# Relative attention with a max-of-three layer on one core: the first tiles between the bias groups, a new place for the weight conversion, another count of products with v

## The chip, the cores and the metric

The kernel runs on one core of one Trainium2 chip. The metric is the device time of one execution in microseconds, as the median of several runs; the profile is one such execution.

## The reference

Four batches, eight heads, 576 positions, head dimension 64. A small network of 32 hidden units makes a bias for each pair of positions and each head; attention with that bias is followed by a layer that takes the largest of three products.

```python
scores = scale * np.matmul(q, k.transpose(0, 1, 3, 2))
x = (np.log1p(np.abs(rel)) / psi_i)[..., None]
bias = np.maximum(x @ w1 + b1, 0.0) @ w2                 # 576 x 576 x 8
attn = softmax(scores + bias)                            # over the last axis
out = np.matmul(attn, v)                                 # 4 x 8 x 576 x 64
...
h = np.maximum(np.maximum(x @ w1, x @ w2), x @ w3)       # 2304 x 768, x = out as 2304 x 512
return h @ w_out                                         # 2304 x 512
```

## The kernel before

The program is written out in one order by hand; each engine runs its own instructions in that order, and waits where an operand or a buffer is not ready. It has three stages.

**Bias.** 36 groups `g` of 16 rows. `hidden(g)` writes four tiles `hid` (three or four on VectorE, at most one on ScalarE, chosen by a running estimate `load`), `product(g - 1)` multiplies them on TensorE into a PSUM tile `bp`, and `finish` scales that into `bs` on ScalarE or VectorE and writes it to DRAM (`bias_d`). `bp` shares the PSUM tag `s` (two buffers) with the score tiles; `bs` has eight buffers. All DMAs go through SyncE's queue, in order: the write of each group, the reads `load_bias` of five bias tiles (`bias0` to `bias3` with 128 rows, and `biasm` with the last 64) when their groups are written, and the loads of q, k and v. The reads are issued at g = 10, 18, 26 and 34 and after the last group.

**Attention.** A unit is a pair of heads of one batch (16 units); a unit has five tiles t = 0 to 4, the last with one head's width. `step(n)` issues, in this order: `front(n)` (scores of tile n of `sched`, 12 matmuls, 6 for t = 4, into two `s` tiles), some queued products with v, `shift` (VectorE: scores plus bias, and their minimum) and `expo` (ScalarE: exponent and sum) for each head, `norm(n - 1)` (VectorE: a reciprocal; POOL: the scaling of e), for t = 0 and 1 a part of `prep` for the next unit (k, then q: a cast to the high part on ScalarE, `kh`/`qh`, and the rest on POOL, `kl`/`ql`), `split_x`, and `flip(n - 5)` (TensorE transposes of e, copied out by ScalarE and VectorE as `et`). Steps 0 to 4 thus have no flip. After tiles 1 and 4 of a unit five pairs of products with v are queued (group 0 over tiles 0 and 1, group 1 over tiles 2 to 4); steps with n mod 5 = 0, 1, 2, 3, 4 issue 3, 2, 2, 2, 1 of them. The accumulator `pv` has a single PSUM buffer. `split_x` copies a finished `pv` into `xhi` and `xlo` on VectorE, two instructions; the first pair of a new group calls it as well. Step 0 stands behind the last bias group, steps 1 to 84 after the bias stage.

**Max of three.** From 345 us on, matmuls with weights that `convert` has turned from double precision to two parts, with seven VectorE instructions per weight tile. The first three weight tiles (`load_w(..., 0)`) are converted during attention: from step 23 on, each third step advances the conversion by two pieces, behind the flip's copies.

Of the kernel before, what the change touches and what calls it, by code (L numbers as in the profile page):

```python
# [19 lines left out]
def kernel(  # L20
# [66 lines left out]
    def bias_stage(pool):  # L87
# [41 lines left out]
        for g in range(NG + 1):  # L129
            if g < NG:  # L130
                hidden(g)
            if g:
                product(g - 1)
            for x in range(max(g - 2, 0), g if g == NG else g - 1):
                finish(pool, k, load, x, late.pop(x))
            yield
# [33 lines left out]
    TS = 2  # L170
    sched = [(un, t) for un in range(len(units)) for t in range(NS)]
    NSTEP = len(sched)
    LAG = NS

    class Attention:
        def __init__(self, pool):
            self.pool = pool
            self.data = {}
            self.st = {}
            self.et = {}  # L180
            self.pvq = []
            self.done = []
            self.vl = [pool.tile([128, 2, D], F32, name=f"vl{x}", bufs=1) for x in range(2)]
# [14 lines left out]
        def prep(self, un):  # L198
            pool, u = self.pool, self.data[un]
            for w in "kq":  # L200
# [4 lines left out]
                nc.scalar.copy(hi, r)  # L205
                nc.gpsimd.tensor_tensor(out=lo, in0=r, in1=hi.bitcast(F32), op=ALU.subtract)
                yield
# [12 lines left out]
        def heads(self, n):  # L220
            return 2 if sched[n][1] < NTQ else 1

        def front(self, n):
            un, t = sched[n]
            pool, u = self.pool, self.data[un]
# [15 lines left out]
        def shift(self, n, h):  # L241
            un, t = sched[n]
            pool, st = self.pool, self.st[n]
# [9 lines left out]
        def expo(self, n, h):  # L253
            pool, st = self.pool, self.st[n]
            if h == 0:
                st["e"] = pool.tile([128, 2 * S], F32, tag="e", bufs=NS + 1, name=f"e{n}")
                st["sm"] = pool.tile([128, 2], F32, tag="sm", bufs=NS + 1, name=f"sm{n}")
            sn, nm = st.pop(h)
# [6 lines left out]
        def norm(self, n):  # L265
            st, nh = self.st[n], self.heads(n)
            sm = st["sm"][:, 0:nh]
            rc = self.pool.tile([128, 2], F32, tag="rc", bufs=NS + 1, name=f"rc{n}")
            nc.vector.reciprocal(rc[:, 0:nh], sm)  # L269
# [5 lines left out]
        def flip(self, n):  # L275
            un, t = sched[n]
            pool, e2 = self.pool, self.st[n]["e"]
            g = 0 if t < TS else 1
# [7 lines left out]
            tps = []  # L286
            for h in range(self.heads(n)):
                tp = ps_t(f"tp{un}_{t}_{h}")
# [47 lines left out]
        def step(self, n, more=None):  # L336
            m, f = n - 1, n - LAG
            nh = 0
            if n < NSTEP:
                un, t = sched[n]  # L340
                hp, b = units[un]
                if t == 0 and un + 2 < len(units):
                    self.load_qk(un + 2)
                if t == 2 and un:
                    self.load_v(un)
                nh = self.heads(n)
                self.front(n)
            for _ in range((3, 2, 2, 2, 1)[n % NS]):
                if self.pvq:
                    self.pvq.pop(0)()  # L350
            back = 0 <= f < NSTEP
            for h in range(nh):
# [12 lines left out]
            if back:  # L365
# [3 lines left out]
                if len(tps) > 1:  # L369
                    nc.vector.tensor_copy(*tps[1])  # L370
            if more is not None:
                for _ in range(2):
                    next(more, None)
            if back:
                un, t = sched[f]
                g = 0 if t < TS else 1
                w = 128 * TS if g == 0 else S - 128 * TS
                del self.st[f]
                if t in (TS - 1, NS - 1):
                    self.queue_pv(un, 128 * TS * g, w, *self.et)  # L380


    def convert(pool, src, hi, lo, name):
        n = src.shape[1] * src.shape[2] // 2
# [28 lines left out]
    def load_w(pool, wpool, f):  # L413
        for i, m in enumerate((mw1, mw2, mw3)):
# [3 lines left out]
            src = m[:, 256 * f:256 * f + 256].rearrange("(c p) f -> p c f", p=128)  # L418
            yield from convert(wpool, src, hi, lo, f"{i}_{f}")

# [71 lines left out]
    with tc.manual_schedule():  # L492
# [9 lines left out]
        with tc.tile_pool(name="bias_p", bufs=1) as bp:  # L502
            for g, _ in enumerate(bias_stage(bp)):
# [17 lines left out]
        xlo.extend(xpool.tile([128, NT], F32R, name=f"xlo{i}") for i in range(HP))  # L521
        w0 = load_w(wpool, wpool, 0)
# [66 lines left out]
```

## Time and profile before

| | |
|---|---|
| median of three runs | 643.92 us (643.84 to 645.93) |
| the profiled execution, own time | 646.02 us |
| its span, first to last instruction | 644.2 us |
| TensorE busy | 610.4 us |
| VectorE, ScalarE, POOL busy | 382.5, 297.3, 164.4 us |

The profiled execution took 2.1 us more than the median, and 1.8 us of its time lie outside the span. TensorE is busy in 95% of the span. From 345 us on it has no idle time to speak of; the idle time lies in the bias stage, in the first steps of attention and in the waits of its units.

### The profile page before, as it was taken

To read this page: it belongs to the slowest core of one execution; us is meant where nothing else is said; L and a number is where in the kernel's file an instruction comes from. 1 tells how busy PE (TensorE), PEld (TensorE's weight loads), DVE (VectorE), ACT (ScalarE), POOL (GpSimd) and SP (SyncE) were. 2 spreads that over 40 slices of the span, in tenths; PEclk is the share of its full clock that TensorE was granted. 3 is DMA by queue.
4 is the path that set the end of the run, shared out by engine and by line. 5 is a ranking of instruction groups with operands and counts; after the bars stand their busy time and mean duration, and the time that the engine had idled before them with its cause. 6 is when DMAs were issued, how large, how long until landed. Compare 5 with 4: busy or idle time off the path is not lost.

```text
span 644.2 us, 11473 instructions
## 1 busy us (share of the span) xinstructions
PE 610.4 (95%) x4248; PEld 464.2 (72%) x4248; DVE 382.5 (59%) x948; ACT 297.3 (46%) x788; POOL 164.4 (26%) x186
## 2 busy tenths in 40 slices
PE   8987799999899989999999999999999999999998
PEld 4324566666566666666666898989889898988886
DVE  7985466666686777678644474646646473233331
ACT  7977677776767667768651000000000001034443
POOL 2403555555556556656430000000000000000000
PEclk9989699999899999999999999999999999999999
DMA  5868323632264224510011111212212110001111
GB/s 166 274 234 291 108 60 102 180 88 59 52 180 138 61 62 132 173 33 19 20 33 34 34 65 44 75 46 67 65 34 83 48 66 0 1 34 66 66 65 67
DMA packets 47863, 55.16 MB, mean 86 GB/s; under 512 B 21952, under 2 KB 31424, under 8 KB 47808
## 3 DMA queue, kind: packets, MB, share of 16 engines
q1 hardware_dynamic: 47808, 54.43, 27.4%
q8 instruction: 34, 0.56, 0.4%
q14 instruction: 21, 0.17, 0.1%
HBM read 38.81 MB, written 15.61 MB: 84 GB/s over the span
## 4 chain that ended last, share of the span: by engine, by line
PE 72%; ACT 14%; DVE 6%; issue 4%; DMA 2%; POOL 1%; SPq 0%; DVEq 0%; ACTq 0%
PE pv L320 10%; PE h L461 8%; PE h L462 8%; PE h L463 8%; PE tp L291 7%; PE s L237 6%; ACT e L259 6%; PE g L462 4%; PE g L463 4%; PE g L461 4%; PE o L486 4%; PE o L485 4%; PE o L487 4%; ACT bs L144 2%; ACT et L367 2%
## 5 line engine op out<-in xcount | busy, mean ns | idle before, releaser
L259 ACT ACTIVATE e<-sn,nm 128x576 f32<-128x576 f32 x144 | 110.8, 770 | 70.5 <-DVE nm L247 54.3
L272 POOL TENSOR_SCALAR e<-e,rc 128x576 f32<-128x576 f32 x144 | 106.9, 755 | 99.4 <-DVE rc L269 66.6
L468 ACT COPY m<-h 128x512 f32<-128x512 f32 (+1 forms) x30 | 16.3, 544 | 206.1 <-PE h L463 187.2
L247 DVE CUSTOM_DVE_ANT_0 sn<-s,bias 128x576 f32<-128x576 f32 x128 | 91.8, 754 | 28.8 <-PE s L237 28.8
L320 PE MATMUL pv<-et,vt 128*64 128x320 f32 (+1 forms) x512 | 78.1, 420 | 15.8 <-ACT et L367 15.6
L463 PE MATMUL h<-xhi,wl 128*128 128x512 f32 (+1 forms) x240 | 88.3, 368 | 0.0
L461 PE MATMUL h<-xhi,wh 128*128 128x512 f32 (+1 forms) x240 | 88.2, 368 | 0.0
L462 PE MATMUL h<-xlo,wh 128*128 128x512 f32 (+1 forms) x240 | 88.2, 368 | 0.0
L291 PEld LDWEIGHTS tp<-ident,e 128*128 128x128 f32 x576 | 63.1, 143 | 34.1 <-issue 22.5
L291 PE MATMUL tp<-ident,e 128*128 128x128 f32 x576 | 82.3, 285 | 0.0
L370 DVE COPY et<-tp 128x512 f32<-128x512 f32 x64 | 44.0, 687 | 54.2 <-PE tp L291 52.0
L237 PE MATMUL s<-kh,qh 64*128 64x288 f32 (+1 forms) x288 | 64.1, 352 | 8.2 <-DVE nm L247 7.4
L320 PEld LDWEIGHTS pv<-et,vt 128*64 128x64 f32 x512 | 34.6, 136 | 39.5 <-ACT et L367 23.3
L237 PE MATMUL s<-kl,qh 64*128 64x288 f32 (+1 forms) x288 | 53.6, 305 | 0.0
L237 PEld LDWEIGHTS s<-kh,qh 64*128 64x128 f32 (+1 forms) x288 | 35.7, 190 | 23.4 <-DVE nm L247 12.3
L237 PE MATMUL s<-kh,ql 64*128 64x288 f32 (+1 forms) x288 | 51.7, 297 | 0.0
L367 ACT COPY et<-tp 128x512 f32<-128x512 f32 x80 | 45.8, 573 | 9.3 <-PE tp L291 9.3
L440 DVE TENSOR_TENSOR hl<-ht,hh 128x128 fp32r<-128x128 f32 x108 | 23.4, 285 | 44.9 <-ACT hh L439 44.9
L461 PEld LDWEIGHTS h<-xhi,wh 128*128 128x128 f32 x240 | 45.1, 188 | 6.2 <-issue 0.5
L469 DVE TENSOR_TENSOR m<-h,m 128x512 f32<-128x512 f32 (+1 forms) x30 | 19.1, 638 | 50.9 <-ACT m L468 50.8
L462 PEld LDWEIGHTS h<-xlo,wh 128*128 128x128 f32 x240 | 45.0, 188 | 5.7
L463 PEld LDWEIGHTS h<-xhi,wl 128*128 128x128 f32 x240 | 45.0, 188 | 5.6
(75 smaller groups left out, 1058.3 us busy)
## 6 DMA issues: line engine op xcount, KB each, us to landing
bias_d<-bs SPq DMA_DIRECT2D x36, 295.5 KB, 5.2
bias<-bias_d SPq DMA_DIRECT2D x16, 576.0 KB, 3.9
w<-in_moe_w_dram SPq DMA_DIRECT2D x18, 512.0 KB, 3.5
qr<-in_qd_dram SPq DMA_DIRECT2D x16, 320.0 KB, 3.1
kr<-in_kd_dram SPq DMA_DIRECT2D x16, 320.0 KB, 3.7
out_dram<-ot SPq DMA_DIRECT2D x17, 256.0 KB, 2.0
vt<-in_v_dram SPq DMA_DIRECT2D x32, 128.0 KB, 2.5
w64o<-in_moe_w_out_dram SPq DMA_DIRECT2D x6, 512.0 KB, 3.2
```

The source lines that it names most:

```text
L237: nc.tensor.matmul(ss[h][:, x, 0:HALF], lhsT=u[q][p, r], rhs=u[k][p, c:c + HALF], start=(j == 0), stop=(j == 2))
L247: nc.vector.tensor_tensor_reduce(out=sn.rearrange("p (a b) -> p a b", a=2), in0=st["s"][h][:, :, 0:HALF], in1=bt.rearrange("p (a b) -> p a ...
L259: nc.scalar.activation(st["e"][:, S * h:S * h + S], sn, ACTF.Exp, scale=-1.0, bias=nm, accum_out=st["sm"][:, h:h + 1])
L272: nc.gpsimd.tensor_scalar(out=e, in0=e, scalar1=rc[:, h:h + 1], scalar2=1.0, op0=ALU.mult, op1=ALU.mult)
L291: nc.tensor.transpose(tp[:, 128 * c:128 * c + 128], e2[:, k0:k0 + 128], ident)
L320: nc.tensor.matmul(pv[p], lhsT=w, rhs=x, start=(c == 0), stop=(c == NTQ))
L367: nc.scalar.copy(*tps[0])
L370: nc.vector.tensor_copy(*tps[1])
L461: nc.tensor.matmul(o, lhsT=hi[:, r], rhs=x, start=(c == 0), stop=False)
L462: nc.tensor.matmul(o, lhsT=hi[:, r], rhs=y, start=False, stop=False)
L463: nc.tensor.matmul(o, lhsT=lo[:, r], rhs=x, start=False, stop=(c == KDM - 1))
L485: nc.tensor.matmul(po, lhsT=hh[:, f], rhs=woh[:, f, r], start=(f == 0), stop=False)
```

## The change

Three tiles of unit 0 are issued between bias groups, behind g = 17, 25 and 33 (`AMID`); there `finish` also takes the group just multiplied. The steps follow a new list `fronts`: tiles 0, 1, 2 of unit 0, then tiles 0, 1, 2 of unit 1, then tiles 3 and 4 of unit 0, then 3 and 4 of unit 1, and so on in the old order. `flip` keeps the old order. So step 3 stands behind the last bias group, and steps 3 and 4 alone come after it without a flip. `norm` makes up for the first steps two at a time from step 3 on. `prep` computes the low parts of units 0 and 1 on VectorE; that of unit 1 stands in steps 1 and 2, that of unit 2 as a whole in step 8. Products with v are issued 1, 3, 2, 2, 2 per step. The conversion of the first weights advances by one piece in steps with n mod 5 of 2, 3 and 4 from step 20 on, right behind `expo`, and its last two pieces go to ScalarE and POOL. e has eight buffers instead of six, and v is loaded a tile later.

```diff
-            for x in range(max(g - 2, 0), g if g == NG else g - 1):
-                finish(pool, k, load, x, late.pop(x))
+            for x in sorted(late):
+                if x < g - 1 or g in AMID or g == NG:
+                    finish(pool, k, load, x, late.pop(x))
...
+    AMID = (17, 25, 33)
+    fronts = [sched[x] for x in (0, 1, 2, 5, 6, 7, 3, 4)] + sched[8:]
...
                 nc.scalar.copy(hi, r)
-                nc.gpsimd.tensor_tensor(out=lo, in0=r, in1=hi.bitcast(F32), op=ALU.subtract)
+                eng = nc.vector if un < 2 else nc.gpsimd
+                eng.tensor_tensor(out=lo, in0=r, in1=hi.bitcast(F32), op=ALU.subtract)
...
-                st["e"] = pool.tile([128, 2 * S], F32, tag="e", bufs=NS + 1, name=f"e{n}")
+                st["e"] = pool.tile([128, 2 * S], F32, tag="e", bufs=NS + 3, name=f"e{n}")
...
-            m, f = n - 1, n - LAG
+            f = n - LAG
             nh = 0
             if n < NSTEP:
-                un, t = sched[n]
+                un, t = fronts[n]
...
-                if t == 2 and un:
+                if t == 3 and un:
                     self.load_v(un)
...
-            for _ in range((3, 2, 2, 2, 1)[n % NS]):
+            for _ in range((1, 3, 2, 2, 2)[n % NS]):
                 if self.pvq:
                     self.pvq.pop(0)()
...
                 self.expo(n, h)
+            if more is not None:
+                next(more, None)
             if n < NSTEP and b == B - 1 and hp + 1 < HP:
                 load_bias(hp + 1, t)
-            if 0 <= m < NSTEP:
-                self.norm(m)
+            for _ in range(2 if n >= len(AMID) else 0):
+                if self.normed < min(n, NSTEP):
+                    self.norm(self.normed)
+                    self.normed += 1
             if n < NSTEP and un + 1 < len(units):
-                if t == 0:
+                t0 = (1, 3)[un] if un < 2 else 0
+                if t == t0:
                     self.splits = self.prep(un + 1)
-                if t < 2:
-                    next(self.splits)
+                for _ in range(2 if un == 1 else 1):
+                    if t0 <= t < t0 + 2:
+                        next(self.splits, None)
             self.split_x()
...
-            if more is not None:
-                for _ in range(2):
-                    next(more, None)
...
-        nc.vector.tensor_copy(hi, a)
+        if split is None:
+            nc.vector.tensor_copy(hi, a)
+            yield
+            nc.vector.tensor_tensor(out=lo, in0=a, in1=hi.bitcast(F32), op=ALU.subtract)
+        else:
+            nc.scalar.copy(hi, a)
+            nc.gpsimd.tensor_tensor(out=lo, in0=a, in1=hi.bitcast(F32), op=ALU.subtract)
         yield
-        nc.vector.tensor_tensor(out=lo, in0=a, in1=hi.bitcast(F32), op=ALU.subtract)
-        yield
...
-                if g >= NG:
+                if g in AMID or g >= NG:
                     at.step(n)
...
-            at.step(n, w0 if n >= NSTEP - 57 and n % 3 == 0 else None)
+            at.step(n, w0 if n >= NSTEP - 60 and n % NS >= 2 else None)
```

What the move does to the engines' order is shown at three places. In the rows a name carries its group or unit and tile: `hid106` is a hidden tile of g = 26, `sn1_0` the shift of step 1 for head 0, `s2_0_0` the scores of unit 2, tile 0, head 0, `pv0_256` the products of unit 0, group 1, and `pv1_0` those of unit 1, group 0.

First VectorE at the 25th bias group, before:

```order
L106 TENSOR_SCALAR hid106_654<-sm0_93,bp_96 128x432 [waits DVE_49,PE_49]
L106 TENSOR_SCALAR hid105_656<-sm0_93,bp_96 128x432 [waits DVE_49]
L106 TENSOR_SCALAR hid104_658<-sm0_93,bp_96 128x432 [waits DVE_49]
L147 TENSOR_SCALAR bs24_669<-bp24_640,sm0_93 128x591 [waits DMAHW2_49,DMAHW7_49,PE_49,Activation_49]
L106 TENSOR_SCALAR hid110_675<-sm0_93,bp_96 128x448 [waits DVE_49]
L106 TENSOR_SCALAR hid109_677<-sm0_93,bp_96 128x448 [waits DVE_49]
```

and in the change:

```order
L106 TENSOR_SCALAR hid100_667<-sm0_93,bp_96 128x416 [waits DVE_49]
L148 TENSOR_SCALAR bs24_681<-bp24_669,sm0_93 128x591 [waits DMAHW2_49,PE_49]
L254 ISA sn1_0_698,nm1_0_699<-s0_1_0_684,bias1_86 128x576 [waits DMAHW5_49,PE_49]
L254 ISA nm1_0_699 128x1
L254 ISA sn1_1_704,nm1_1_705<-s0_1_1_685,bias1_86 128x576 [waits PE_49,Activation_49]
L254 ISA nm1_1_705 128x1
L213 TENSOR_TENSOR kl1_710<-kr1_467,kh1_709 128x640 [waits DMAHW0_49,Activation_49]
L106 TENSOR_SCALAR hid106_715<-sm0_93,bp_96 128x432 [waits DVE_49]
L106 TENSOR_SCALAR hid105_717<-sm0_93,bp_96 128x432 [waits DVE_49]
```

The hidden tiles of g = 26 stood ahead of `bs24`; now they stand behind it, behind both shifts and behind `kl1`, which waits for a cast of ScalarE.

Second TensorE in step 12, before:

```order
L237 MATMUL s2_2_1_1399<-kl2_1078,qh2_1126 128x288
L237 MATMUL s2_2_0_1398<-kh2_1077,ql2_1127 128x288
L237 MATMUL s2_2_1_1399<-kh2_1077,ql2_1127 128x288
L320 MATMUL pv1_0_1412<-et1_0_1323,vt1_1145 64x256 [waits DMAHW0_49,DVE_49,Activation_49]
L320 MATMUL pv1_0_1412<-et1_0_1323,vt1_1145 64x256 [waits DMAHW2_49,DVE_49]
L320 MATMUL pv1_0_1412<-et1_0_1323,vt1_1145 64x256 x2
```

and in the change:

```order
L244 MATMUL s2_2_1_1390<-kl2_1226,qh2_1229 128x288
L244 MATMUL s2_2_0_1389<-kh2_1225,ql2_1230 128x288
L244 MATMUL s2_2_1_1390<-kh2_1225,ql2_1230 128x288
L327 MATMUL pv0_256_1298<-et0_1_1172,vl0_81 64x320 x2
L327 MATMUL pv1_0_1407<-et1_0_1319,vt1_1188 64x256 [waits DVE_49,DMAHW0_49,PE_49,Activation_49]
L327 MATMUL pv1_0_1407<-et1_0_1319,vt1_1188 64x256 [waits DMAHW2_49]
```

The last pair of the old group and the first pair of the new one, which stood a step apart, now follow each other.

Third VectorE at the same place, before:

```order
L269 RECIPROCAL rc10_1368<-sm10_1309 128x2 [waits Activation_49,Pool_49]
L330 CAST xhi0_928<-pv0_256_1298 128x320 [waits PE_49]
L331 TENSOR_TENSOR xlo0_932<-pv0_256_1298,xhi0_928 128x320 [waits DVE_49]
L370 COPY et1_0_1323<-tp1_1_1_1383 128x4x128 [waits PE_49]
L247 ISA sn12_0_1417,nm12_0_1418<-s2_2_0_1398,bias2_87 128x576 [waits PE_49]
```

and in the change:

```order
L276 RECIPROCAL rc10_1366<-sm10_1305 128x2 [waits Activation_49,Pool_49]
L383 COPY et1_0_1319<-tp1_1_1_1379 128x4x128 [waits PE_49]
L337 CAST xhi0_1019<-pv0_256_1298 128x320 [waits PE_49]
L338 TENSOR_TENSOR xlo0_1023<-pv0_256_1298,xhi0_1019 128x320 [waits DVE_49]
L254 ISA sn12_0_1410,nm12_0_1411<-s2_2_0_1389,bias2_87 128x576
```

`xhi` and `xlo` moved from ahead of the copy of step 11 to a place directly ahead of the shift of step 12.

## Rows read from the trace of the kernel before

**Rows 1.** The page: busy time of the engines (us, share of the span, instructions); and from the waits of TensorE over the whole span the largest sum (us in total, times, longest).

```profile
PE 610.4 (95%) x4248; PEld 464.2 (72%) x4248; DVE 382.5 (59%) x948; ACT 297.3 (46%) x788; POOL 164.4 (26%) x186
...
PE pv L320 <- ACT et L367: 15.6, 30, 1.3
```

**Rows 2.** Four stretches of 2 us in the bias stage and the first steps: busy us (instructions) of PE, PEld, DVE, ACT and POOL, then the granted clock, the share of the DMA engines and GB/s.

```profile
40.00:42.00 2.00, 0.00 (x0) 0.00 (x0) 2.00 (x7) 0.61 (x1) 0.00 (x0) 0.88 1.07 398
42.00:44.00 2.00, 1.81 (x16) 0.66 (x20) 0.71 (x2) 1.93 (x4) 0.00 (x0) 0.50 0.99 359
44.00:46.00 2.00, 2.00 (x32) 0.83 (x28) 1.49 (x4) 1.51 (x3) 0.00 (x0) 0.77 0.97 322
...
62.00:64.00 2.00, 1.90 (x12) 1.59 (x12) 0.65 (x3) 1.76 (x5) 2.00 (x2) 0.50 1.05 385
```

**Rows 3.** Bias stage, from the timeline: start us, us, engine, line, operation, tiles, count, and in brackets the idle time before and what ended it. PE's products, three of ScalarE's `bs` (groups 22, 23 and 25), VectorE's hidden tiles (three a group), and POOL's `kl` of unit 0.

```profile
13.29 7.75 POOL L206 TENSOR_TENSOR kl<-kr,kh 128x640 fp32r<-128x640 f32 x1 [11.24 <-ACT kh L205]
...
24.00 15.47 PE L127 MATMUL bp<-hid,w2s 128*32 128x223 f32 x224 [0.59 <-DVE bs L147]
...
35.23 0.75 ACT L144 ACTIVATE bs<-bp,sm 128x591 f32<-128x591 f32 x1
...
36.40 0.76 ACT L144 ACTIVATE bs<-bp,sm 128x591 f32<-128x591 f32 x1
...
41.39 0.75 ACT L144 ACTIVATE bs<-bp,sm 128x591 f32<-128x591 f32 x1 [3.13 <-DMA bias_d<-bs]
...
42.19 10.75 PE L127 MATMUL bp<-hid,w2s 128*32 128x447 f32 x152 [2.73 <-ACT bs L144]
...
44.44 6.45 DVE L106 TENSOR_SCALAR hid<-sm,bp 128x512 f32<-128x512 f32 x15 [1.74 <-PE bp L127]
```

**Rows 4.** The first steps, timeline: the fronts of steps 0 and 1 (second head), the shift and exponent of step 0, the cast and the low part of k for unit 1, the shift of step 4, and the first products with v in step 7.

```profile
55.22 0.40 PE L237 MATMUL s<-kh,qh 64*128 64x288 f32 x1 [0.56 <-ACT bs L144]
...
56.19 0.76 DVE L247 CUSTOM_DVE_ANT_0 sn<-s,bias 128x576 f32<-128x576 f32 x1 [2.18 <-PE s L237]
...
56.99 0.77 ACT L259 ACTIVATE e<-sn,nm 128x576 f32<-128x576 f32 x1 [1.83 <-DVE nm L247]
...
57.69 0.40 PE L237 MATMUL s<-kh,qh 64*128 64x288 f32 x1 [0.28 <-DVE nm L247]
...
58.76 0.71 ACT L205 CAST kh<-kr 128x640 fp32r<-128x640 f32 x1
...
59.54 1.56 POOL L206 TENSOR_TENSOR kl<-kr,kh 128x640 fp32r<-128x640 f32 x1 [36.88 <-ACT kh L205]
...
68.99 0.76 DVE L247 CUSTOM_DVE_ANT_0 sn<-s,biasm 128x576 f32<-128x576 f32 x1 [3.24 <-DMA biasm<-bias_d]
...
79.38 1.15 PE L320 MATMUL pv<-et,vt 128*64 128x256 f32 x8 [1.32 <-ACT et L367]
```

**Rows 5.** Units of attention, PE's timeline: the first products of group 0 in steps 12, 17 and 22, between the last two of them a front, two pairs of group 0, a flip and three pairs of group 1; then the first products of group 0 in step 77.

```profile
95.99 1.15 PE L320 MATMUL pv<-et,vt 128*64 128x256 f32 x8 [0.57 <-ACT et L367]
...
112.60 1.15 PE L320 MATMUL pv<-et,vt 128*64 128x256 f32 x8 [0.57 <-ACT et L367]
...
114.82 0.40 PE L237 MATMUL s<-kh,qh 64*128 64x288 f32 x2
...
115.81 1.08 PE L320 MATMUL pv<-et,vt 128*64 128x256 f32 x8
116.82 1.09 PE L291 MATMUL tp<-ident,e 128*128 128x128 f32 x8
...
121.35 1.84 PE L320 MATMUL pv<-et,vt 128*64 128x320 f32 x12 [0.16 <-ACT et L367]
...
129.21 1.15 PE L320 MATMUL pv<-et,vt 128*64 128x256 f32 x8 [0.56 <-ACT et L367]
...
321.11 1.15 PE L320 MATMUL pv<-et,vt 128*64 128x256 f32 x8
```

**Rows 6.** The end of attention, timeline: the last pair of a group 1 in step 81, the two instructions that copy it out of PSUM, and the first pair of the next group.

```profile
333.34 0.71 PE L320 MATMUL pv<-et,vl 128*64 128x320 f32 x4
...
334.10 0.49 DVE L330 CAST xhi<-pv 128x320 fp32r<-128x320 f32 x1 [0.66 <-PE pv L320]
334.62 0.49 DVE L331 TENSOR_TENSOR xlo<-pv,xhi 128x320 fp32r<-128x320 f32 x1
...
335.31 1.62 PE L320 MATMUL pv<-et,vt 128*64 128x256 f32 x8
```

**Rows 7.** Conversion, timeline: an instruction of it on VectorE, and the front behind whose banks the shift after it was late; the same instruction later, with POOL idle; and from the groups of lines VectorE's subtraction of two SBUF tiles.

```profile
235.58 1.92 DVE L403 SCALAR_TENSOR_TENSOR wa<-w,signm,wt 128x512 uint32<-128x512 uint32 x1
...
238.90 0.39 PE L237 MATMUL s<-kh,qh 64*128 64x288 f32 x1 [0.28 <-DVE nm L247]
...
348.05 0.75 DVE L403 SCALAR_TENSOR_TENSOR wa<-w,signm,wt 128x512 uint32<-128x512 uint32 x1
...
L408 DVE TENSOR_TENSOR wl<-wa,wh 128x512 fp32r<-128x512 f32 x18 | 13.0, 720 | 0.5
```

**Rows 8.** Two long waits of TensorE in a unit, timeline: products with v in steps 32 and 47, and the transposes behind the first.

```profile
163.96 1.72 PE L320 MATMUL pv<-et,vt 128*64 128x256 f32 x8 [1.31 <-ACT et L367]
165.61 1.97 PE L291 MATMUL tp<-ident,e 128*128 128x128 f32 x8
...
218.24 1.16 PE L320 MATMUL pv<-et,vt 128*64 128x256 f32 x8 [1.32 <-ACT et L367]
```

More of the change, by code (lines that the diff above doesn't have):

```diff
@@ L182, in __init__ @@
             self.done = []
+            self.normed = 0
             self.vl = [pool.tile([128, 2, D], F32, name=f"vl{x}", bufs=1) for x in range(2)]
@@ L220, in heads @@
         def heads(self, n):
-            return 2 if sched[n][1] < NTQ else 1
+            return 2 if fronts[n][1] < NTQ else 1
         def front(self, n):
-            un, t = sched[n]
+            un, t = fronts[n]
             pool, u = self.pool, self.data[un]
@@ L241, in shift @@
         def shift(self, n, h):
-            un, t = sched[n]
+            un, t = fronts[n]
             pool, st = self.pool, self.st[n]
@@ L255, in expo @@
             if h == 0:
-                st["e"] = pool.tile([128, 2 * S], F32, tag="e", bufs=NS + 1, name=f"e{n}")
-                st["sm"] = pool.tile([128, 2], F32, tag="sm", bufs=NS + 1, name=f"sm{n}")
+                st["e"] = pool.tile([128, 2 * S], F32, tag="e", bufs=NS + 3, name=f"e{n}")
+                st["sm"] = pool.tile([128, 2], F32, tag="sm", bufs=NS + 3, name=f"sm{n}")
             sn, nm = st.pop(h)
@@ L267, in norm @@
             sm = st["sm"][:, 0:nh]
-            rc = self.pool.tile([128, 2], F32, tag="rc", bufs=NS + 1, name=f"rc{n}")
+            rc = self.pool.tile([128, 2], F32, tag="rc", bufs=NS + 3, name=f"rc{n}")
             nc.vector.reciprocal(rc[:, 0:nh], sm)
@@ L276, in flip @@
             un, t = sched[n]
-            pool, e2 = self.pool, self.st[n]["e"]
+            pool, e2 = self.pool, self.st.pop(fronts.index((un, t)))["e"]
             g = 0 if t < TS else 1
@@ L286, in flip @@
             tps = []
-            for h in range(self.heads(n)):
+            for h in range(2 if t < NTQ else 1):
                 tp = ps_t(f"tp{un}_{t}_{h}")
@@ L336, in step @@
         def step(self, n, more=None):
-            m, f = n - 1, n - LAG
+            f = n - LAG
             nh = 0
             if n < NSTEP:
-                un, t = sched[n]
+                un, t = fronts[n]
                 hp, b = units[un]
@@ L377, in step, with convert @@
                 w = 128 * TS if g == 0 else S - 128 * TS
-                del self.st[f]
                 if t in (TS - 1, NS - 1):
                     self.queue_pv(un, 128 * TS * g, w, *self.et)
-    def convert(pool, src, hi, lo, name):
+    def convert(pool, src, hi, lo, name, split=None):
         n = src.shape[1] * src.shape[2] // 2
@@ L405, in convert, with load_w @@
         yield
-        nc.vector.tensor_copy(hi, a)
-        yield
-        nc.vector.tensor_tensor(out=lo, in0=a, in1=hi.bitcast(F32), op=ALU.subtract)
+        if split is None:
[5 more added lines that the diff above has]
+            nc.gpsimd.tensor_tensor(out=lo, in0=a, in1=hi.bitcast(F32), op=ALU.subtract)
         yield
     wf = {}
-    def load_w(pool, wpool, f):
+    def load_w(pool, wpool, f, split=None):
         for i, m in enumerate((mw1, mw2, mw3)):
@@ L418, in load_w @@
             src = m[:, 256 * f:256 * f + 256].rearrange("(c p) f -> p c f", p=128)
-            yield from convert(wpool, src, hi, lo, f"{i}_{f}")
+            yield from convert(wpool, src, hi, lo, f"{i}_{f}", split)
     def moe(pool, wpool):
@@ L521 @@
         xlo.extend(xpool.tile([128, NT], F32R, name=f"xlo{i}") for i in range(HP))
-        w0 = load_w(wpool, wpool, 0)
+        w0 = load_w(wpool, wpool, 0, True)
         while n < NSTEP + LAG:
-            at.step(n, w0 if n >= NSTEP - 57 and n % 3 == 0 else None)
+            at.step(n, w0 if n >= NSTEP - 60 and n % NS >= 2 else None)
             n += 1
@@ L544 @@
     from concourse.bass_utils import run_bass_kernel_spmd
-    nc = bacc.Bacc("TRN2", target_bir_lowering=False, num_devices=1)
+    nc = bacc.Bacc("TRN2", target_bir_lowering=False, num_devices=1, dynamic_dma_scratch_size=1024)
     B, H, S, D = inputs["q"].shape
```

## The prediction

> **What bounds the kernel now.** I read the busy times and TensorE's waits first. TensorE is busy for 610 of 644 us and the other engines for at most 59% of the span, so time is lost or won where TensorE stands still; the largest sum is its wait for `et` ahead of products with v, 15.6 us in 30 pieces [rows 1]. Then the timeline, stretch by stretch. Three places matter. In the bias stage ScalarE writes a group every 1.17 us (35.23 to 36.40), TensorE needs 1.1 (15.47 us for 14 groups of 16 matmuls) and VectorE 1.29 for its three hidden tiles (6.45 for 15): all three are full, until a `bs` buffer waits for its DMA at 41.39 and everything stops for 3 us [rows 3], after which the clock is at 0.50 for 3 us [rows 2]. In the first steps there is nothing but fronts and softmax: a front each 2.47 us (55.22 to 57.69), a wait of 3.24 us for `biasm`, and the first product with v at 79.38, 24.2 us after the first tile's front [rows 4]; the clock is at 0.50 there too, its lower level [rows 2]. In a unit without conversion TensorE is the bound: 16.61 us from 112.60 to 129.21, with two waits of 0.57 and 0.16 [rows 5]. The 13 units from step 12 to step 77 took 225.1 us (95.99 to 321.11), 9.2 more than 13 such units.
>
> **First steps: what is removed.** After the bias stage two steps without a flip remain: 2 x 2.47 = 4.9 from step 3's front to step 5's [rows 4]. Step 5 is bound by its two shifts, 2.5. Step 6's flip waits for the PSUM buffer that ScalarE empties behind two exponents, so 2.9. From step 7's front to its first product pass 1.0 for the front (114.82 to 115.81) and 0.5 for the copy. Together 11.8 instead of 24.2: **-12.4**. The `biasm` wait goes, since step 7 comes some 10 us behind the last group.
>
> **First steps: what is added to the bias stage.** The order shows the price: at g = 25 the next hidden tiles stand behind both shifts and `kl1`. From the start of `bs22`: 0.75 until its bank is free, 1.1 for product 24, 0.75 for `bs24`, and 0.97 until the shift (55.22 to 56.19) make 3.6; the exponents start 0.8 later and the cast 1.77 after them (56.99 to 58.76), 6.2; the cast takes 0.71, 6.9; `kl1` is not there on VectorE before, its nearest row is a subtraction of 512 columns in 0.72 [rows 7], so 0.9 for 640; three hidden tiles 1.3; product 26 1.1. `bs26` starts at 10.2, and without the tile it starts at 4 x 1.17 = 4.7. So 5.5, and 5.5 again at g = 33 with `ql1`. At g = 17 no cast stands there, ScalarE makes its hidden tile at 6.2 and the product ends at 7.8 against 4.5: 3.3. Sum 14.3. The bounds: nothing is hidden (14.3), or only ScalarE's own work counts (3 x 1.77 + 2 x 0.71 = 6.7). I take the upper, since all three engines drain at each tile, less the DMA stop, which now falls into a tile: 3.1 and 0.6 for the two groups behind it at half clock. TensorE stands still for some 3.6 us behind each of the last two tiles, longer than the 2.73 us that brought the clock to 0.50 [rows 2, 3]; two products each at half speed, partly hidden by ScalarE's pitch, cost 1.0 a tile. 14.3 - 3.7 + 2.0 = **+12.6**. Moving `kl0` and `ql0` to VectorE costs 1.8 there, and frees it from POOL's two, of which the first took 7.75 us against 1.56 alone [rows 3, 4]; I set this at nothing, as VectorE is two groups ahead at that time, and at -1 to +1 if not. Steps 3 to 6 are again half idle, so that the clock falls as it did at 62 us: **+0.7** (0 to 1.5).
>
> The loads of unit 2's q and k now stand in SyncE's queue ahead of the read of `bias1`, and the writes behind it wait as well; that read waits for its groups' writes anyway, so I cost it at nothing, and at 2 to 4 us if the second tile has to wait.
>
> **Step 8.** `prep` of unit 2 is issued whole, two steps ahead of its use. From step 8's shift: casts at 2.6, done at 3.9; POOL's `kl2` and `ql2`, 1.56 each, one behind the other, from 3.4 to 6.5. TensorE would be at step 10's front at 4.4 (rest of step 8 2.1, step 9 2.3) and needs `ql2` after 0.3; ScalarE's copy for step 9's flip stands behind both casts, too. **+2.0** (0.5 to 3).
>
> **The units.** With 1, 3, 2, 2, 2 the last pair of group 1 and the first pair of the next group 0 are neighbours in the same step, and `pv` has one buffer: the first pair waits for `xhi` and `xlo` of the last. The trace has that chain once: from the last pair at 333.34 to the next at 335.31 1.97 us, or 1.83 if TensorE goes on 0.06 after `xlo` [rows 6]; less 0.61 for the pair itself (1.84 for three) it is a wait of 1.2 to 1.35. What the new count saves is 0.57 (the last pair covers that copy) and 0.16 (step 4 has a pair more ahead of it). A clean unit is then 16.61 - 0.73 + 1.2 = 17.1; measured by the fronts, the two waits are 0.85, which gives 16.95. I take 17.05: **+0.4** for unit 0. The shift of this step starts 1.5 us later, but its banks are free again 0.4 before the next front.
>
> **Conversion.** It costs 9.2 us over 13 units now, because two pieces in front of a shift make that late: 1.92 us at 235.58, then a front waiting at 238.90 [rows 7]. Behind `expo` one piece at a time, of 0.75 alone, ends before the next shift's scores are there (some 1.4 us after the second shift), and in two of five steps conversion pauses. I leave 1 us for ScalarE's copy and POOL's subtraction. 13 x 17.05 + 1 = 222.7 against 225.1: **-2.4**.
>
> On a neighbouring point the Trainium skill speaks against this edit. The instruction at 235.58 ran 1.92 us while the same form took 0.75 with POOL idle [rows 7]. SBUF — State Buffer, section "Who interferes with whom", says that VectorE and POOL hold one port pair by turns, each for a whole instruction, in certain modes and with two SBUF inputs; the trace agrees. By it each of the 15 pieces may still run into a POOL scaling, and my sum would be 2 to 8 us higher.
>
> **End of attention.** Step 82 has the new wait of 1.25 without a front, step 80 loses 0.5 of its own: **+0.7**.
>
> **Sum.** -12.4 + 12.6 + 0.7 + 2.0 + 0.4 - 2.4 + 0.7 = +1.6. The profiled execution would have a span of 645.8 and an own time of 647.6; it lay 2.1 above the median, so the median comes out at 645.5, which is no change that can be measured: 0.5%, 3.2 us, is about what tells one from none here.
>
> **The rivals.**
> - *The tiles fit into the bias stage.* VectorE runs ahead, so the drains overlap and only ScalarE's 6.7 us less the stop of 3.1 are paid, with some for the clock: about 5.5 instead of 12.6, 638.5. For it: ScalarE idles 3 us at the stop. Against: the order, which puts hidden tiles behind the shifts. 0.18.
> - *The units gain more.* If `xlo` is out sooner than in that one row, or long waits hang on conversion alone, a unit takes 16.5: 13 x 0.55 = 7 less, 638.4. Against: both instructions are in the order. 0.08.
> - *Slower: the clock falls in the units.* The new wait of 1.2 stands in one piece. At 163.96 a wait of 1.31 was followed by products of 1.72 and transposes of 1.97 instead of 1.15 and 1.09: 1.4 us lost; at 218.24 a wait of 1.32 was followed by products of 1.16 [rows 5, 8]. If it falls in five of 15 units, 7 us, 652.5; from two on it decides. 0.15.
> - *Slower: conversion still collides with POOL*, 0.8 us on the path in ten steps (pieces in the last two of each unit's steps, 1.17 longer, 0.4 hidden): 653. 0.10.
> - *Slower: the second tile waits for its bias read*, 4 us: 649.5. 0.09.
>
> **How the numbers follow.** My forecast has 0.40, all of it within 0.5%. The first two rivals are faster, 0.26, the last three slower, 0.34. For the range I take 638 to 653, which leaves out the far ends of the rivals, some 2 in 10; the forecast's own range is 642.5 to 648.5, from the bounds of step 8, clock and `pv` wait.
>
> **What the changed profile would show.** Step 3's front of the second head near 68 us (before, step 0's at 55.2); first product with v near 80; a wait of TensorE for `ql` of 1 us or more at step 10; in each unit one wait of 1.2 us for `xlo` at the first product of group 0 and none of `et`; 17.0 us a unit; no front late because of conversion. I am wrong if step 3 comes before 64 us, if units differ from 17.05 by more than 0.3, or if the clock shows 0.5 inside the units.

## The result, and the profile after

| | before | after |
|---|---|---|
| median | 644.56 us (643.84 to 645.93, 4 runs) | 653.69 us (651.31 to 655.09, 4 runs) |
| ratio | | 1.0137 (95% interval 1.0112 to 1.0161) |
| profiled execution, own time and span | 646.02, 644.2 us | 651.31, 649.5 us |

The change made the kernel 9.1 us slower. The forecast was 645.5 us, no change that can be measured, with a range that ends at 653.

The waits of TensorE in after over the whole span (us in total, times, longest), to be read beside [rows 1]:

```profile
PE pv L327 <- DVE xlo L338: 20.5, 15, 1.5
PE bp L127 <- DVE hid L106: 10.2, 6, 3.5
PE pv L327 <- ACT et L380: 2.2, 4, 0.8
```

The 15.6 us of waiting for `et` are down to 2.2. In their place stand 20.5 us for `xlo`, and 10.2 us for hidden tiles in the bias stage, where before only one wait for them, of 0.3 us, was left.

The bias stage of after, timeline: `bs` of groups 16, 18, 24, 32 and 35; `kl1` on VectorE; the two products that waited longest; the front of step 3 (second head).

```profile
28.50 0.83 DVE L148 TENSOR_SCALAR bs<-bp,sm 128x591 f32<-128x591 f32 x1 [0.97 <-ACT bs L145]
34.92 0.74 ACT L145 ACTIVATE bs<-bp,sm 128x591 f32<-128x591 f32 x1
41.54 0.83 DVE L148 TENSOR_SCALAR bs<-bp,sm 128x591 f32<-128x591 f32 x1 [2.12 <-PE bp L127]
46.70 0.82 DVE L213 TENSOR_TENSOR kl<-kr,kh 128x640 fp32r<-128x640 f32 x1 [1.86 <-ACT kh L211]
48.74 9.54 PE L127 MATMUL bp<-hid,w2s 128*32 128x431 f32 x120 [3.32 <-DVE hid L106]
58.35 0.83 DVE L148 TENSOR_SCALAR bs<-bp,sm 128x591 f32<-128x591 f32 x1 [1.60 <-PE bp L127]
65.75 3.52 PE L127 MATMUL bp<-hid,w2s 128*32 128x512 f32 x48 [3.51 <-DVE hid L106]
69.33 0.75 ACT L145 ACTIVATE bs<-bp,sm 128x591 f32<-128x591 f32 x1 [1.36 <-PE bp L127]
70.13 0.40 PE L244 MATMUL s<-kh,qh 64*128 64x288 f32 x1 [0.33 <-ACT bs L145]
```

The same five `bs` in the trace of the kernel before:

```profile
28.55 0.75 ACT L144 ACTIVATE bs<-bp,sm 128x591 f32<-128x591 f32 x1
30.66 0.75 ACT L144 ACTIVATE bs<-bp,sm 128x591 f32<-128x591 f32 x1 [0.44 <-PE bp L127]
37.37 0.83 DVE L147 TENSOR_SCALAR bs<-bp,sm 128x591 f32<-128x591 f32 x1
50.92 0.76 ACT L144 ACTIVATE bs<-bp,sm 128x591 f32<-128x591 f32 x1
54.41 0.75 ACT L144 ACTIVATE bs<-bp,sm 128x591 f32<-128x591 f32 x1 [1.36 <-PE bp L127]
```

Up to group 16 both are level (28.50 and 28.55). That doesn't make `kl0` and `ql0` on VectorE free, since the change also writes group 16 a place earlier in its order: two runs below that differ in this stage by the engine of the low parts alone come to group 16 at 27.95 and 27.80, five with them on VectorE at 28.50 to 29.02, some 0.7 us later. Behind group 16 each tile sets the stage back: groups 16 to 18 take 6.42 instead of 2.11 us, 24 to 32 take 16.81 instead of 13.55 (the second tile, with the DMA stop of before inside), 32 to 35 take 10.98 instead of 3.49. That is 4.3, 3.3 and 7.5 us. At 46.70 VectorE had waited 1.86 us for ScalarE's cast before it could make `kl1`; the hidden tiles stand behind it, and TensorE waits for them until 48.74.

Attention in after, timeline: the first product with v; step 9's transpose and step 10's front; then, at step 12, the last pair of group 1, `xhi`, `xlo` and the first pair of group 0; and the latter in step 77.

```profile
81.70 1.15 PE L327 MATMUL pv<-et,vt 128*64 128x256 f32 x8 [0.84 <-ACT et L380]
89.69 0.33 PE L309 MATMUL lp<-swap,e 128*128 128x128 f32 x1 [0.60 <-ACT et L381]
91.54 0.40 PE L244 MATMUL s<-kh,ql 64*128 64x288 f32 x2 [0.95 <-POOL ql L213]
98.97 0.76 PE L327 MATMUL pv<-et,vl 128*64 128x320 f32 x4
99.80 0.49 DVE L337 CAST xhi<-pv 128x320 fp32r<-128x320 f32 x1 [1.14 <-PE pv L327]
100.33 0.49 DVE L338 TENSOR_TENSOR xlo<-pv,xhi 128x320 fp32r<-128x320 f32 x1
101.08 0.65 PE L327 MATMUL pv<-et,vt 128*64 128x256 f32 x4 [1.35 <-DVE xlo L338]
...
326.11 0.65 PE L327 MATMUL pv<-et,vt 128*64 128x256 f32 x4 [1.38 <-DVE xlo L338]
```

From these and [rows 4, 5] the span divides like this: the first product comes 2.3 us later (81.70 against 79.38); unit 0 takes 19.38 instead of 16.61, 2.8 more; the 13 units take 225.03 instead of 225.12; the rest 0.3 more. Together 5.3, the difference of the spans. The other 3.8 us of the 9.1 lie between these two executions and their medians: that of before was 1.5 above its own, that of after 2.4 below. The first experiment shows where.

The change's program also sets `dynamic_dma_scratch_size=1024`, which its description leaves out. No run varies this alone; the run on the kernel before with a later load of v (below) does without it and has the same units as the changed kernel with the same count (15.70 and 15.71 us).

### The profile page after: what moved, and what is told of

Same layout as the page of the kernel before. It is cut to its first block, busy times and chain, and to the rows that moved or that the text cites. A ratio compares the mean times of both kernels' runs of the same rounds, so it can differ in the third digit from the quotient of the medians.

```text
span 649.5 us, 11395 instructions
## 1 busy us (share of the span) xinstructions
PE 603.6 (93%) x4248; PEld 456.2 (70%) x4248; DVE 374.7 (58%) x946; ACT 297.7 (46%) x791; POOL 153.7 (24%) x185
## 4 chain that ended last, share of the span: by engine, by line
PE 87%; DVE 5%; ACT 3%; issue 2%; DMA 1%; POOL 1%; DVEq 0%; POOLq 0%; ACTq 0%
PE pv L327 14%; PE s L244 11%; PE tp L298 11%; PE h L474 8%; PE h L476 8%; PE h L475 8%; PE g L476 4%; PE g L475 4%; PE g L474 4%; PE o L500 4%; PE o L498 4%; PE o L499 4%; PE bp L127 4%; DVE hid L106 2%; ACT e L266 1%
## 5 line engine op out<-in xcount | busy, mean ns | idle before, releaser
L327 PE MATMUL pv<-et,vt 128*64 128x320 f32 (+1 forms) x512 | 79.4, 420 | 22.7 <-DVE xlo L338 20.5
L298 PEld LDWEIGHTS tp<-ident,e 128*128 128x128 f32 x576 | 61.5, 141 | 33.9 <-issue 29.9
L298 PE MATMUL tp<-ident,e 128*128 128x128 f32 x576 | 80.7, 280 | 0.1
L327 PEld LDWEIGHTS pv<-et,vt 128*64 128x64 f32 x512 | 30.5, 136 | 52.0 <-issue 36.2
L244 PE MATMUL s<-kh,qh 64*128 64x288 f32 (+1 forms) x288 | 58.8, 344 | 4.2 <-DVE nm L254 2.0
L127 PE MATMUL bp<-hid,w2s 128*32 128x79 f32 (+48 forms) x640 | 44.7, 414 | 12.9 <-DVE hid L106 10.2
L244 PE MATMUL s<-kl,qh 64*128 64x288 f32 (+1 forms) x288 | 49.6, 295 | 0.0
L244 PE MATMUL s<-kh,ql 64*128 64x288 f32 (+1 forms) x288 | 48.6, 291 | 1.0 <-POOL ql L213 1.0
```

What stands on the lines that cost most here:

```text
L127: nc.tensor.matmul(bp[32 * c:32 * c + 32, o:o + w], lhsT=w2s, rhs=src, start=True, stop=True)
L244: nc.tensor.matmul(ss[h][:, x, 0:HALF], lhsT=u[q][p, r], rhs=u[k][p, c:c + HALF], start=(j == 0), stop=(j == 2))
L298: nc.tensor.transpose(tp[:, 128 * c:128 * c + 128], e2[:, k0:k0 + 128], ident)
L327: nc.tensor.matmul(pv[p], lhsT=w, rhs=x, start=(c == 0), stop=(c == NTQ))
```

## The experiments

All times in us. Each ratio is to runs of the kernel before that were made beside the run (medians 643.45, 644.47 and 644.61).

**The changed kernel a second time.**

> The changed kernel as it is, for a second profile and more times. Theory (its first profiled execution was the fastest of four because the clock stayed high after the bias stage): in a usual execution the clock is at 0.50 in two of the steps 3 to 6, the first product with v comes near 84.3 us instead of 81.70, and nothing else differs; median 653 to 654. Rival (the units run slower in the other executions, with a clock that falls at the wait for xlo): units above 17.3 us and a granted clock below 1 between 100 and 340 us.

654.47, ratio 1.0153 (1.0124 to 1.0182). A stretch of 2 us behind the bias stage, and the units as one stretch: busy times by engine, the granted clock, DMA share, GB/s. First the first profile of after, then this run:

```profile
76.00:78.00 2.00, 2.00 (x19) 1.60 (x18) 1.95 (x6) 1.36 (x5) 2.00 (x4) 1.00 0.43 96
100.00:340.00 240.00, 220.01 (x1868) 150.59 (x1868) 163.04 (x441) 173.66 (x479) 131.99 (x152) 1.00 0.32 90
```

```profile
76.00:78.00 2.00, 2.00 (x15) 1.72 (x14) 0.87 (x3) 0.94 (x4) 2.00 (x4) 0.50 0.70 171
100.00:340.00 240.00, 220.15 (x1875) 150.71 (x1875) 163.02 (x440) 174.19 (x481) 133.94 (x154) 1.00 0.32 91
```

This run's timeline: the front of step 3, the first product, and that of group 0 in step 12:

```profile
70.80 0.39 PE L244 MATMUL s<-kh,qh 64*128 64x288 f32 x1 [0.56 <-ACT bs L145]
...
83.67 1.15 PE L327 MATMUL pv<-et,vt 128*64 128x256 f32 x8 [1.30 <-ACT et L380]
...
103.05 0.65 PE L327 MATMUL pv<-et,vt 128*64 128x256 f32 x4 [1.35 <-DVE xlo L338]
```

The theory holds in the main, with a smaller figure: the clock fell to its lower level behind the bias stage, where it had stayed at the upper one in the first profile, and the first product came 2.0 us later. Of these, 1.3 lie behind the front of step 3; the other 0.7 are there at that front already (70.80 against 70.13), which the theory didn't have: in this run the clock was at 0.50 from 32 to 34 us as well, behind the first tile, where the first profile has 1.00. From the first product on everything is as in the first profile (19.38 for unit 0, clock 1.00 in the units). Three more profiles below run the same instructions up to this product; over all five it comes at 81.70, 83.67, 84.34, 85.98 and 86.01. The first profile of after was a lucky one. Four profiles with the bias stage and first steps of the kernel before show 77.18, 77.99, 78.05 and 79.38; that of before was an unlucky one. Middle against middle, that is median against median of these executions, the first product is 6.3 us later, not 2.3, and 6.3 + 2.8 - 0.1 + 0.3 = 9.3 stands against the measured 9.1. That they meet so closely is in part luck, as the five lie 4.3 us apart and the four 2.2.

**The old count of products in the changed kernel.**

```diff
-            for _ in range((1, 3, 2, 2, 2)[n % NS]):
+            for _ in range((3, 2, 2, 2, 1)[n % NS]):
```

> The changed kernel with the old count of products with v, 3, 2, 2, 2, 1; all else as changed. Theory (the wait for the bank of pv sets the unit): a unit goes back from 17.26 us to about 16.6, as in the kernel before, the wait for xlo (20.5 us in 15 pieces) is gone, and waits of 0.57 and 0.16 us for et stand in its place; 15 units x 0.65 = 9.8 us less, a median near 644. Rival (the old waits come back larger, since conversion pieces now stand in three of five steps): a unit stays at 17.0 or more and the median at 650 to 654.

644.86, ratio 1.0009 (0.9991 to 1.0027): the loss is gone. Waits of TensorE, and the first products of group 0 in two units:

```profile
PE pv L327 <- ACT et L380: 11.6, 22, 1.3
```

```profile
102.78 1.15 PE L327 MATMUL pv<-et,vt 128*64 128x256 f32 x8 [0.56 <-ACT et L380]
119.33 1.15 PE L327 MATMUL pv<-et,vt 128*64 128x256 f32 x8 [0.56 <-ACT et L380]
```

A unit takes 16.55 us, and the wait for `xlo` is no longer in the list. So the new count costs about 0.7 us a unit, 9 in all.

**A count that leaves a step between the two groups.**

```diff
-            for _ in range((1, 3, 2, 2, 2)[n % NS]):
+            for _ in range((1, 3, 1, 3, 2)[n % NS]):
```

> The changed kernel with the count 1, 3, 1, 3, 2: the last pair of group 1 still covers the copy of et in step n mod 5 = 2, but the first pair of the next group 0 comes a step later, when xhi and xlo are out. Theory: both waits are gone, that of 1.35 us for xlo and those of 0.57 and 0.16 us for et; a unit takes 17.26 - 1.35 = 15.9 us, 15 x 1.35 = 20 us less than the changed kernel, a median near 634. Rival (VectorE or ScalarE then bounds a unit, or the flip of that step waits for its PSUM buffers instead): a unit at 16.6 or more, a median of 643 or more.

631.99, ratio 0.9816 (0.9791 to 0.9840). The first products of group 0 in two units, and VectorE's copies of the group 1 ahead of the second:

```profile
121.33 1.52 PE L327 MATMUL pv<-et,vt 128*64 128x256 f32 x12
137.04 1.51 PE L327 MATMUL pv<-et,vt 128*64 128x256 f32 x12
```

```profile
135.76 0.47 DVE L337 CAST xhi<-pv 128x320 fp32r<-128x320 f32 x1
136.27 0.49 DVE L338 TENSOR_TENSOR xlo<-pv,xhi 128x320 fp32r<-128x320 f32 x1
```

`xlo` ends at 136.76, TensorE needs the bank at 137.04, and neither wait is left: 15.71 us a unit, 1.55 less than with the changed count and 0.9 less than before. This confirms the mechanism from the other side: the last pair of group 1 does cover the copy of `et`, and only the pair right behind it pays.

**The conversion alone, on the kernel before.**

```diff
+            if more is not None:
+                next(more, None)
             if n < NSTEP and b == B - 1 and hp + 1 < HP:
...
-            if more is not None:
-                for _ in range(2):
-                    next(more, None)
...
-            at.step(n, w0 if n >= NSTEP - 57 and n % 3 == 0 else None)
+            at.step(n, w0 if n >= NSTEP - 60 and n % NS >= 2 else None)
```

with `convert`'s last two pieces on ScalarE and POOL as in the change.

> The kernel before with the new place of the conversion alone (one piece behind expo in steps with n mod 5 of 2, 3 and 4, the last two on ScalarE and POOL). Theory: the 9.2 us that conversion cost over 13 units fall to 1 or less, a median 8 to 9 us below the kernel before, near 636. Rival (it is the new count of products that keeps conversion from costing anything, by the pair that covers the copy of et): the gain is 4 us or less.

635.46, ratio 0.9882 (0.9861 to 0.9902), 8.0 us. The first products of group 0 around one unit with conversion in it:

```profile
226.71 1.15 PE L320 MATMUL pv<-et,vt 128*64 128x256 f32 x8 [0.56 <-ACT et L369]
243.33 1.15 PE L320 MATMUL pv<-et,vt 128*64 128x256 f32 x8 [0.56 <-ACT et L369]
```

16.62 us with conversion, 16.61 without [rows 5]. The 13 units from step 12 to step 77 take 215.91 us (93.79 to 309.70) instead of 225.12, which is 13 x 16.61: conversion costs nothing there, and the gain doesn't hang on the count.

The pieces themselves ran shorter too. One of its instructions on VectorE between 100 and 320 us (count, us in all, mean ns), first in before, then in this run:

```profile
L403 DVE SCALAR_TENSOR_TENSOR wa<-w,signm,wt 128x512 uint32<-128x512 uint32 x3 | 3.4, 1140 | 0.0
```

```profile
L402 DVE SCALAR_TENSOR_TENSOR wa<-w,signm,wt 128x512 uint32<-128x512 uint32 x3 | 2.3, 772 | 0.0
```

In after the mean is 749, and the longest of all 15 pieces on VectorE is 755. In program order a piece now stands ahead of the reciprocal for which POOL's scaling waits: in after a piece starts at 174.31, the reciprocal at 174.92 and POOL at 175.24.

**No tiles in the bias stage.**

```diff
-    AMID = (17, 25, 33)
-    fronts = [sched[x] for x in (0, 1, 2, 5, 6, 7, 3, 4)] + sched[8:]
+    AMID = ()
+    fronts = sched
```

> The changed kernel without tiles between the bias groups: the old order of fronts, one norm a step, step 0 behind the last group; counts, conversion and the place of the low parts of k and q as changed. Theory: the first product with v comes near 79.4 us as in the kernel before, 2.3 us sooner than 81.70, and the span is 2 to 3 us less than the changed kernel's. Rival (moving the tiles gains by itself and the low parts on VectorE are what costs): the first product comes at 82 us or later and the median rises.

649.18, ratio 1.0088 (1.0068 to 1.0108), 4.5 below the changed kernel, more than the 2 to 3 expected from its first profile. The first product:

```profile
78.11 1.15 PE L327 MATMUL pv<-et,vt 128*64 128x256 f32 x8 [0.64 <-ACT et L380]
```

It comes as in the kernel before (77.18 to 79.38), and 6.2 ahead of the middle of the five with tiles; this execution was 1.6 below the median of its kernel, which is most of what 6.2 and 4.5 differ by. So the tiles in the bias stage are a loss, and the low parts of k and q on VectorE, without tiles around them, show no cost beyond the 2.2 us by which those four differ.

**The low parts of k and q on POOL in the changed kernel.**

```diff
-                eng = nc.vector if un < 2 else nc.gpsimd
+                eng = nc.gpsimd
```

> The changed kernel with all low parts of k and q on POOL as in the kernel before, so that no hidden tile stands behind a subtraction that waits for ScalarE's cast. Theory: of the 3.32 and 3.51 us that TensorE waits for hidden tiles behind the second and third tile, the part behind the cast and the subtraction goes: VectorE goes on 44.84 instead of 47.52, 2.7 us sooner, twice; the waits of 1.30 for a hidden tile at 14.6 and 19.3 go as well. Step 3 comes 4 to 5 us sooner and the median is 4 us below the changed kernel's 653.7. Rival (ScalarE's own work at a tile, two exponents and the cast, sets the stop, whoever subtracts): TensorE then waits for bs or for ScalarE's hidden tile instead, step 3 comes less than 1.5 us sooner, and the median falls by less than 1.5.

650.40, ratio 1.0083 (1.0062 to 1.0103), 3.3 below the changed kernel. The product behind the second tile, the front of step 3 and the first product; `bs` of groups 24, 32 and 35; then POOL's `kl1`:

```profile
45.52 0.92 PE L127 MATMUL bp<-hid,w2s 128*32 128x431 f32 x6 [0.63 <-DVE hid L106]
...
64.95 0.40 PE L244 MATMUL s<-kh,qh 64*128 64x288 f32 x1 [0.56 <-ACT bs L145]
...
78.68 1.15 PE L327 MATMUL pv<-et,vt 128*64 128x256 f32 x8 [1.30 <-ACT et L380]
```

```profile
41.00 0.83 DVE L148 TENSOR_SCALAR bs<-bp,sm 128x591 f32<-128x591 f32 x1 [2.12 <-PE bp L127]
55.45 0.83 DVE L148 TENSOR_SCALAR bs<-bp,sm 128x591 f32<-128x591 f32 x1 [0.63 <-PE bp L127]
64.15 0.75 ACT L145 ACTIVATE bs<-bp,sm 128x591 f32<-128x591 f32 x1 [0.76 <-PE bp L127]
```

```profile
46.21 1.65 POOL L213 TENSOR_TENSOR kl<-kr,kh 128x640 fp32r<-128x640 f32 x1 [22.64 <-ACT kh L211]
```

The wait behind the second tile falls from 3.32 to 0.63, and step 3 comes 5.2 us sooner than in the first profile of after. Groups 24 to 32 take 14.45 instead of 16.81, and 32 to 35 take 8.70 instead of 10.98: the subtraction that waited for the cast was 2.4 of the second tile's 3.3 us and 2.3 of the third's 7.5. ScalarE's own work alone did not set the stop, but what makes up the other 5.2 of the third tile, and the 4.3 of the first, no run takes apart. The first product is then about where it is without tiles, since fewer steps follow the bias stage. The median fell by less than the 4 expected.

**The low part of unit 2's k on VectorE.**

```diff
-                eng = nc.vector if un < 2 else nc.gpsimd
+                eng = nc.vector if un < 2 or (un == 2 and w == "k") else nc.gpsimd
```

> The changed kernel with the low part of unit 2's k on VectorE; that of q stays on POOL. Theory (POOL's two subtractions of 1.54 us, one behind the other, are late for step 10): the low part of q starts when its cast is done, 1 us sooner, and the wait of 0.95 us for it at 91.54 is gone; the unit from the first product to step 12's falls from 19.38 to 18.4. Rival (ScalarE's casts in front of the copies are what is late): the wait of 0.60 for lp stays and the unit is at 19 or more. On the median 1 us or nothing.

655.03, ratio 1.0150 (1.0126 to 1.0175): nothing gained, a miss. VectorE's `kl2`, and TensorE in steps 9 and 10:

```profile
92.70 0.83 DVE L213 TENSOR_TENSOR kl<-kr,kh 128x640 fp32r<-128x640 f32 x1 [1.85 <-ACT kh L211]
```

```profile
93.92 0.63 PE L298 MATMUL tp<-ident,e 128*128 128x128 f32 x4 [1.11 <-ACT et L380]
96.52 0.76 PE L327 MATMUL pv<-et,vt 128*64 128x320 f32 x4 [0.62 <-ACT et L380]
```

The wait for `ql` is gone, and waits for copies, 1.11 and 0.62, stand in its place; unit 0 takes 19.33 instead of 19.38. The rival is right about the unit, though the wait of 0.60 that it named is gone. By the order of the trace two casts in one step keep ScalarE from its copies, and VectorE, which waits 1.85 us for the cast, holds up the copy and the shift behind it; no run takes these two apart.

**Conversion and the new count on the kernel before.** As the run with the conversion alone, and:

```diff
-            for _ in range((3, 2, 2, 2, 1)[n % NS]):
+            for _ in range((1, 3, 1, 3, 2)[n % NS]):
```

> The kernel before with the new place of the conversion and the count 1, 3, 1, 3, 2; bias stage, order of tiles and low parts as before. Theory: the parts add up; a unit falls from 16.61 to 15.70 as in the run with this count, 15 x 0.91 = 13.6 us below 635.5 of the conversion alone, a median near 622. Rival (without the tiles ahead the steps have less slack and the copies come late): a unit at 16.2 or more, a median of 629 or more.

656.04, ratio 1.0179 (1.0151 to 1.0207), a miss of 34 us. Waits of TensorE:

```profile
PE pv L320 <- DMA vl<-in_v_dram: 18.8, 23, 2.4
```

The kernel before loads v of a unit at t = 2, which with this count stands ahead of the last pair of the unit two before it, and both use the same `vl`. That pair waits for the load, and it multiplies with the later unit's rows: that part of the computation is changed here, and the time shows only what the wait costs. So "v is loaded a tile later", which the prediction passed over, belongs to the count; in the change, too, that last pair stands in step n mod 5 = 2.

**The same with v loaded a tile later.**

```diff
-                if t == 2 and un:
+                if t == 3 and un:
```

> As the run before it with the conversion moved and the count 1, 3, 1, 3, 2 on the kernel before, but with v loaded a tile later, as in the changed kernel. Without that, the load of v for unit u + 2 stands ahead of the last pair that reads vl of unit u, so that this pair waited for the load (18.8 us in 23 pieces) and read the later unit's rows. Theory: those waits are gone, a unit takes 15.7 us and the median is near 622, 13.6 below the conversion alone. Rival (the last pair still meets a load, or the copies come late without tiles ahead): a unit at 16.2 or more, a median of 629 or more.

623.42, ratio 0.9665 (0.9640 to 0.9690): faster than both kernels, by 21 and 30 us. The front of step 0, the first product, and those of group 0 in two units:

```profile
55.05 0.40 PE L237 MATMUL s<-kh,qh 64*128 64x288 f32 x1 [0.57 <-ACT bs L144]
...
77.99 0.72 PE L320 MATMUL pv<-et,vt 128*64 128x256 f32 x4 [1.32 <-ACT et L369]
...
96.26 1.52 PE L320 MATMUL pv<-et,vt 128*64 128x256 f32 x12
...
111.96 1.51 PE L320 MATMUL pv<-et,vt 128*64 128x256 f32 x12
```

15.70 us a unit; the gains of conversion and count add up.

**Tiles, low parts on POOL, and that count,** on the changed kernel:

```diff
-            for _ in range((1, 3, 2, 2, 2)[n % NS]):
+            for _ in range((1, 3, 1, 3, 2)[n % NS]):
...
-                eng = nc.vector if un < 2 else nc.gpsimd
+                eng = nc.gpsimd
```

> The changed kernel with all low parts on POOL and the count 1, 3, 1, 3, 2: tiles between bias groups at their cheapest, units at 15.7. Theory (the tiles cost more in the bias stage than they save in the first steps even so, and the two casts in step 8 cost 2): 650.4 - 21.7 = 628.7, some 6 above the kernel before with the same count and conversion. Rival (the tiles pay once the low parts are off VectorE): at or below that kernel.

626.03, ratio 0.9709 (0.9684 to 0.9735). Its first product comes at 77.92:

```profile
77.92 0.72 PE L327 MATMUL pv<-et,vt 128*64 128x256 f32 x4 [1.31 <-ACT et L380]
```

2.6 us above the run before it, less than the 6 expected, but not at or below. Even with the low parts on POOL the tiles only pay for themselves (77.92 against 77.99, one profile each), and step 8's two casts remain to be paid: unit 0 takes 19.72 (77.92 to 97.64) instead of 18.27 (77.99 to 96.26).

## Why the prediction was wrong

The paths through the queues were those forecast, and none of the rivals came about. The steps that failed are the sizes of two terms, both in the same direction: what the tiles and the low clock cost from the bias stage to the first product with v, and the wait for `xlo` in the units.

- **Bias stage, +12.6.** The way through the queues was right: hidden tiles behind shifts, cast and `kl1`. The sum of 14.3 was called the upper bound, and was itself too low: at the first tile, with the clock at 1.00 and no DMA stop, 3.3 were forecast and 4.3 measured; at the third 5.5 and 1.0 for the clock, and 7.5 measured; for the second 5.5 + 1.0 - 3.7 = 2.8 stands against 3.3. That is 15.1 in the first profile. Front of step 3 against step 0's, middle of five (70.13 to 72.36) against middle of four (54.05 to 55.22), it is 16.0 (70.83 - 54.79): 3.4 us mis-sized. `kl0` and `ql0` were set at nothing and cost some 0.7 of it, within the bounds of -1 to +1.
- **First steps, -12.4 and +0.7 for the clock.** With the clock at 1.00 from 72 us on, 11.57 us pass from the front of step 3 to the first product, in the first profile; the sum without a fall of the clock was 11.8, and right. In the other four, with the clock at 0.50 for a part of it, they are 12.87, 13.51, 13.66 and 13.65: the clock cost 1.9 in the middle, not 0.7. And the 24.2 to be saved were those of one execution. Over the four with the old first steps they are 22.7, 22.9, 24.0 and 24.2; the wait for `biasm`, 3.24 us in the profile [rows 4], was 1.75 and 1.98 in two others and wasn't there in the fourth. Saved were 9.7 between the middles (23.2 - 13.5) instead of 11.7, another 2.0. Subtracting, at the end, what that execution lay above its median took care of where the sum starts, not of savings that only this execution had to offer.
- **Units, -2.4.** The chain that costs a unit its wait was named, and from the last pair to the next it measures 2.11 us (98.97 to 101.08), a wait of 1.35 and a unit of 17.26. The trace had 1.97 [rows 6]. It was shaved to 1.83 by letting TensorE go on 0.06 after `xlo`, where the same rows have 0.20 (335.11 to 335.31) and after has 0.26 (100.82 to 101.08); this, averaged with the 0.85 read off the fronts, gave 17.05. With 1.35 and the waits as the rows had them, 0.73, the same sum gives 17.23. Over 13 units 0.21 is 2.7 us; all else in these units took 0.65 and not the 1 left for conversion, so the term is 2.3 short (225.03 against 222.7).
- **Conversion** was right: 8.2 forecast within the units, 9.2 measured there in the run with it alone, 8.0 on the median. By the Trainium skill's rule that VectorE and POOL hold one port pair by turns (SBUF — State Buffer, section "Who interferes with whom"), the prediction put up to 8 us at risk. No run here shows such a loss, and no piece in after was held up: the instruction that took 1.92 us at 235.58 in before [rows 7] takes at most 0.755. That the new place ahead of the reciprocal is what keeps POOL away is read from the order, and not tested apart.
- **Step 8 and unit 0**, +2.0 and +0.4: measured 2.8. The wait for `ql` at step 10 is there (0.95), and so is ScalarE's late copy, which without that wait still leaves unit 0 at 19.33. **End of attention**, +0.7: measured 0.3.
- **Rivals.** The tiles did not fit in more cheaply, and the units gained nothing. The clock in the units is 1.00, so the 1.35 us waits don't lower it. Conversion doesn't collide. Behind the second tile VectorE's shift waited for scores (1.03 us at 43.40), not for `bias1`. Of the prediction's signs of being wrong none came up either (step 3 at 70.13 and not before 64, 17.26 within 0.3 of 17.05, no 0.50 in the units): they were made for another mechanism, not for two sizes.

The range ended at 653 because each slower rival was priced as the only thing to go wrong; two terms short by 5.4 (3.4 and 2.0) and 2.3 us fill nearly the same distance, 8.2 from the forecast to the median, without any of them. The other terms' errors cancel (0.4 each way), which is luck; and the median of before, with a fourth run, lies 0.6 higher.

What stays open is what decides whether an execution keeps its full clock behind the bias stage: the same instructions ran with it at 1.00 and at 0.50. Open is also what a tile costs beyond the subtraction.

## What to carry to other kernels

A single accumulator's price is the whole chain from the last product of one group to the first of the next, here 2.1 us; put other TensorE work of that length between the two groups, and the same move that lost 0.65 us a unit gains 0.9. An instruction that waits for another engine's result doesn't belong ahead of work that a third engine needs, however short it is: here one of 0.82 us cost 2.4 and 2.3. A saving that a profile offers through its own wait or low clock is to be credited only as far as other executions have it too.

## What the hardware showed that was not expected

`kl` on POOL took 7.75 us beside VectorE's hidden tiles in the bias stage of before [rows 3]. In the run with the low parts on POOL `kl0` took 9.25 us at 12.81 beside such tiles, but `kl1` only 1.65 at 46.21, in the same execution. There one hidden tile on VectorE took 1.75 us (at 46.37) instead of the 0.45 of the one behind it, so which of the two engines waits changed from one place to the other. Of two executions of one program, the clock from 76 to 78 us was at its upper level in one (first product 11.57 us behind step 3's front) and at its lower in the other (12.87).
